# Retention followed by an MLP, fp32 on one core: two chunks of retention ahead of the first products, stages skewed, rounding later, another order at the tail

## The chip, the cores and the metric

The kernel runs on one core of a Trainium2 chip. The metric is the device time of one execution in microseconds (us); three runs of the kernel before are given. A core has a matmul engine (PE, with its weight loads shown apart as PEld), a vector engine (DVE), a scalar engine (ACT), GpSimd (POOL) and a sync engine (SP), which here only issues DMAs. Each engine works through its own instructions in order; semaphores order the engines among each other.

## What is computed

A causal retention (attention without softmax, with a decay per head) over 8 batches x 8 heads x 576 positions x 64, whose output, heads side by side, is a matrix x of 4608 tokens x 512. It goes through an MLP with 2048 hidden units:

```python
scores = (1/sqrt(64)) * q @ k.T                       # per batch and head
Dmat   = where(rel >= 0, gamma[h] ** rel, 0)          # gamma[h] = 1 - 2**(-5-h), rel = i - j
x      = ((scores * Dmat) @ v).transpose(0, 2, 1, 3).reshape(4608, 512)
h      = x @ w_in                                     # (4608, 2048)
g      = h * erf(softplus(h))
out    = g @ w_out                                    # (4608, 512)
```

All inputs and the output are float32 where the kernel sees them, except that the two weights arrive as 64-bit floats, whose words the kernel rounds to float32 itself.

## The kernel before, in words

**Retention.** Each batch's 576 positions are cut into pieces of 128, 128, 128, 128 and 64 rows: 40 pieces in all, numbered through. `load(i)` (L107) issues three DMAs on SP's queue for q, k and v of a piece (256 KB each, rows of 64 floats), into pools of 4 buffers. A piece goes through three stages, each a function:

- `transposes(i)`: pops the loaded piece, issues `load(i+3)`, has POOL weigh v of the next piece with its decay (`weigh_values(i+1)`, L252), transposes q and k on PE through an identity (four transposes each, L267), and copies each from PSUM to SBUF on ACT (L269): qT, kT.
- `scores(i)`: 8 score products on PE (L278), and on DVE the causal mask, two instructions into sT (L91, `sT<-s`).
- `outputs(i)`: 8 products sT x v (L290); for pieces that aren't the first of their batch 4 products of q with the running state (L300); for pieces that aren't the last of it 8 products k x v (L312), added to the state by DVE (L91, or copied by ACT at L324 for a batch's first piece). DVE then scales the result into x (L338, four instructions).

All PSUM tiles of these stages come from one pool of four buffers, `ps_at`, so a stage also waits until whoever read the buffer's last content is done. The list `stages` is worked off by `attend`. Its order is transposes(0), scores(0), then for each i: transposes(i+1), outputs(i), scores(i+1).

**Chunks and products.** The tokens are worked on in 9 chunks of 512, the hidden units in 4 groups (g); that gives 36 (g, c) blocks. A block has a `First` (x times w_in) and a `Second` (times w_out). Both use a Strassen-like scheme with 7 half-size products instead of 8, each of four 128x128 by 128x256 float32 matmuls (8 records in the trace). Their operands are sums: `operands_x` makes four sums of x on DVE for a chunk and stores them to DRAM for the later groups (L382); `First.sums` makes the sums of the activations; `sums_in` and `sums_out` make the sums of the weights. `First` runs in the steps first (products A11, A12), middle (S2, S3, S1), last (S4, A22, then Softplus on ACT), `erf` (ACT) and `multiply` (DVE). `Second` runs first (B11, B21), middle (T2, T3, T1) and last (B22, T4), adds its products into the output tile o on DVE, and stores the two halves of the chunk (`store`, L532 for the last group, L529 for the others).

**Weights.** A part is a DMA of 512 KB (L179, 4 buffers). Group 0 has four parts of w_in and four of w_out. Rounding a part is a generator of steps: two ACT instructions (L196, L197); DVE L201; DVE L205; DVE L209; and DVE L214 with two POOL instructions (L215 multiplies, L216 adds), after which the next part's DMA is issued. After the last part of four come four sums of the group on DVE, which need POOL's addition. `round_weights(n)` runs n steps at the place where it is called, so the calls in the main program set where these instructions stand in each engine's order.

**Order.** The order of all instructions is that in which the program issues them (a manual schedule). Before the first product the program runs the stages until chunk 0 is complete (pieces 0 to 3), with two rounding steps after each stage from the second on. Then the seven products of block 0 run with two stages each, then blocks with one stage per product, up to a limit `most` on how far the stages may be ahead. At the end, when no `First` is left, `erf`, middle, last, `multiply`, `sums` and the last `Second` follow.

Of the kernel before, what the change touches and what calls it, by code (L numbers as in the profile page):

```python
# [46 lines left out]
def kernel(  # L47
# [52 lines left out]
    def load(i):  # L100
        if i >= len(pieces):
            return
        b, s0, n = pieces[i]
        t = {}
        for name, src in (("q", q), ("k", k), ("v", v)):
            t[name] = raw.tile([P, H, D], FP32, tag=name, name=f"raw_{name}")
            nc.sync.dma_start(out=t[name][:n], in_=src[b, :, s0 : s0 + n, :].rearrange("h p d -> p h d"))  # L107
        loaded[i] = t

# [6 lines left out]
    gk, gq, gs, tri = (cst[:, a:b] for a, b in zip(ends, ends[1:]))  # L116
    gk = gk.rearrange("p (s h) -> p s h", s=NS)
    gq = gq.rearrange("p (a i) -> p a i", a=NP)
    load(1)
    load(2)  # L120

# [14 lines left out]
    def parts():  # L136


        w2 = w_in.rearrange("(c p) (h f) -> p c h f", p=P, h=2)
        for g in range(n_g):  # L140
            for dc in range(n_dc):
                a = A11 if dc < 2 else A12
                src = w2[:, dc, :, 2 * g * GW : 2 * (g + 1) * GW]
                yield src, "wa", g, a, dc % 2, sums_in if dc == n_dc - 1 else None
            for f in range(2):
                for j in range(GP):
                    ft = f * FH // P + g * GP + j
                    src = w_out[ft * P : (ft + 1) * P, :].rearrange("p (h o) -> p h o", h=2)
                    yield src, "wb", g, B21 if f else B11, j, sums_out if (f, j) == (1, GP - 1) else None

    def sums_in(a11, s3, a12, a22, s1, s2, s4):
        tt(s1, s3, a22, ALU.add)
        yield
        tt(s2, s1, a11, ALU.subtract)
        yield
        tt(s3, a11, s3, ALU.subtract)
        yield
        tt(s4, a12, s2, ALU.subtract)
        yield

    def sums_out(b11, t3, b21, b22, t1, t2, t4):
        tt(t1, t3, b11, ALU.subtract)
        yield
        tt(t2, b22, t1, ALU.subtract)
        yield
        tt(t3, b22, t3, ALU.subtract)
        yield
        tt(t4, b21, t2, ALU.subtract)
        yield

# [11 lines left out]
    def rounding():  # L182


        while words:
            while words[0][2] > most_g[0]:
                yield
            t, name, g, slot, j, sums = words.pop(0)
            w = operands(name, g)
            dst = w[:, slot : slot + 2, j, :]  # L190
            pairs = t[:, :].rearrange("p (h f two) -> p h f two", h=2, two=2)
            pairs_f = t[:, :].bitcast(FP32).rearrange("p (h f two) -> p h f two", h=2, two=2)
            low, high = pairs[:, :, :, 0], pairs[:, :, :, 1]
            r_f, high_f = pairs_f[:, :, :, 0], pairs_f[:, :, :, 1]
            a_f, a = dst, dst.bitcast(UINT32)
            nc.scalar.activation(a_f, high_f, AF.Abs)  # L196
# [19 lines left out]
            nc.gpsimd.tensor_tensor(out=a_f, in0=a_f, in1=r_f, op=ALU.add)  # L216
            load_weights()
            yield
            if sums:
                yield from sums(*(w[:, i] for i in range(7)))  # L220

    for _ in range(4):
        load_weights()
    round_step = rounding()

# [1 line left out]
        for _ in range(n):  # L227
            next(round_step, None)

    ident = cpool.tile([P, P], FP32, name="ident")  # L230
    make_identity(nc, ident)

    states = [cpool.tile([P, NP, P], FP32, name=f"state{j}") for j in range(2)]
    for t in states:
# [24 lines left out]
    def transposes(i):  # L259
        n = pieces[i][2]  # L260
        t = live[i] = loaded.pop(i)
        load(i + 3)
        weigh_values(i + 1)
        for name in "qk":
            pt = ps_at.tile([P, NP, P], FP32, tag="at", name=f"pt_{name}")
            for p in range(NP):
                nc.tensor.transpose(pt[:, p, :n], flat(t[name][:n, 2 * p : 2 * p + 2, :]), ident[:n, :n])  # L267
            t[name + "T"] = att.tile([P, NP, P], FP32, tag=name + "T", name=name + "T")
            nc.scalar.copy(out=t[name + "T"][:, :, :n], in_=pt[:, :, :n])  # L269

    def scores(i):
# [85 lines left out]
    def stages_for(tokens):  # L357
# [99 lines left out]
    class Second:  # L457


        def __init__(self, first):  # L460
            self.of = first
            self.g, self.c = first.g, first.c

        def begin(self):
            self.o = opool.tile([P, 2, 2, D_MODEL], FP32, tag="o", name="o")
# [61 lines left out]
        def store(self, half):  # L527
            if self.g < n_g - 1:
                nc.sync.dma_start(out=od[self.c][:, half], in_=self.o[:, half])  # L529
            else:  # L530
                r0 = self.c * TCH + half * TH
                nc.sync.dma_start(  # L532
                    out=out[r0 : r0 + TH, :].rearrange("(tp p) o -> p tp o", p=P), in_=self.o[:, half]
                )

    order = [(g, c) for g in range(n_g) for c in range(n_ch)]
# [17 lines left out]

    def run(steps, rounds=(), stages=1):

# [83 lines left out]
```

## Time and profile before

| | us |
|---|---|
| three runs | 1096.83, 1097.54, 1098.64 |
| median | 1097.54 |
| profiled execution | 1099.01 |
| span of its instructions | 1097.2 |

| engine | busy us | share of the span |
|---|---|---|
| PE | 1067.0 | 97% |
| PEld (weight loads) | 918.6 | 84% |
| DVE | 618.7 | 56% |
| ACT | 413.2 | 38% |
| POOL | 120.3 | 11% |

The chain of waits that ended last is PE for 90% of the span. Rows of the profile name a source line, an engine, an operation and "tile written <- tiles read", then partitions x elements and the count. A row in order of time starts with its start and its length in us and ends with the idle time of its engine just before it and what ended that. A row of stretches gives the stretch, its length, the busy time of PE, PEld, DVE, ACT and POOL with the number of instructions, the granted clock of PE (1.00 is full), the busy share of the 16 DMA engines (transfers overlap, so it can pass 1) and GB/s. A row of waits gives engine, tile and line, what ended the wait, then the total in us, the number of waits and the longest. L91 is a helper for all tensor-tensor operations of DVE, so there the tile's name counts.

### The profile page before, as it was taken

How to read it: one execution, taken by the hardware profiler on the slowest of the kernel's cores; microseconds unless marked ns; L12 is line 12 of the kernel's file. 1: busy time of each engine (PE TensorE's matmuls, PEld its weight loads, DVE VectorE, ACT ScalarE, POOL GpSimd, SP SyncE). 2: the span in 40 equal slices, each digit the busy share in tenths (PEclk: the TensorE clock that was granted, in tenths of full speed). 3: DMA queues.
4: the chain of work that ended last, by engine and by line, in shares of the span. 5: the costliest groups of instructions: out<-in, count | busy, mean ns of one | idle time of the engine just before them, and what ended most of it. 6: DMA issues, size and time to landing. Idle time of an engine off the chain costs nothing.

```text
span 1097.2 us, 15487 instructions
## 1 busy us (share of the span) xinstructions
PE 1067.0 (97%) x6400; PEld 918.6 (84%) x6400; DVE 618.7 (56%) x1060; ACT 413.2 (38%) x539; POOL 120.3 (11%) x110
## 2 busy tenths in 40 slices
PE   6798999999999999999999999999999999999997
PEld 5686888888888888888888888888888888888885
DVE  3748657576566664455656555565565445445444
ACT  3244433414334134543344344433344433333340
POOL 3323221111111000010000100100011000000000
PEclk8899999999999999999999999999999999999999
DMA  9767466572663343354455543445454333455432
GB/s 242 202 126 195 122 165 156 129 206 90 166 183 83 125 157 141 144 182 163 185 202 208 208 157 145 182 165 205 179 204 149 144 144 144 170 184 193 172 116 76
DMA packets 141126, 178.57 MB, mean 163 GB/s; under 512 B 115200, under 2 KB 115200, under 8 KB 132992
## 3 DMA queue, kind: packets, MB, share of 16 engines
q1 hardware_dynamic: 140912, 177.23, 49.8%
q8 instruction: 50, 0.82, 0.3%
q10 hardware_dynamic: 144, 0.36, 0.1%
q14 instruction: 20, 0.16, 0.0%
HBM read 123.30 MB, written 54.26 MB: 162 GB/s over the span
## 4 chain that ended last, share of the span: by engine, by line
PE 90%; DVE 0%; issue 0%
PE a L473 23%; PE a L394 22%; PE g L473 11%; PE g L394 11%; PE e L473 6%; PE e L394 5%; PE s L278 3%; PE o L290 2%; PE o L300 2%; PE kv L312 1%; PE pt_q L267 1%; PE pt_k L267 1%; DVE o L91 0%; DVE t L91 0%
## 5 line engine op out<-in xcount | busy, mean ns | idle before, releaser
L394 PE MATMUL a<-x,wa 128*128 128x256 f32 x1152 | 276.9, 383 | 0.0
L394 PEld LDWEIGHTS a<-x,wa 128*128 128x128 f32 x1152 | 218.0, 191 | 30.9 <-issue 0.4
L473 PE MATMUL a<-wb,s 128*128 128x256 f32 x864 | 205.8, 381 | 1.6 <-DVE o L91 1.6
L473 PEld LDWEIGHTS a<-wb,s 128*128 128x128 f32 x864 | 162.6, 190 | 25.0 <-DVE o L91 2.4
L91 DVE TENSOR_TENSOR t<-g,t 128x512 f32<-128x512 f32 x72 | 49.7, 691 | 164.0 <-ACT t L424 119.0
L394 PE MATMUL g<-x,wa 128*128 128x256 f32 x576 | 137.2, 381 | 0.0
L91 DVE TENSOR_TENSOR o<-a,o 128x512 f32<-128x512 f32 x108 | 74.2, 687 | 107.0 <-PE a L473 105.2
L394 PEld LDWEIGHTS g<-x,wa 128*128 128x128 f32 x576 | 108.2, 190 | 14.8
L419 ACT COPY t<-a 128x512 f32<-128x512 f32 x36 | 21.1, 585 | 195.7 <-PE a L394 195.7
L215 POOL TENSOR_TENSOR wraw<-wraw 128x512 f32<-128x512 f32 x32 | 34.0, 1063 | 547.5 <-PE a L394 202.8
L91 DVE TENSOR_TENSOR t<-t,s 128x1024 f32<-128x1024 f32 x72 | 86.4, 1241 | 0.0
L436 ACT ACTIVATE s<-t 128x1024 f32<-128x1024 f32 x72 | 72.1, 1048 | 27.9 <-DVE t L91 27.9
L430 ACT COPY t<-a 128x512 f32<-128x512 f32 x36 | 21.1, 586 | 151.2 <-PE a L394 151.2
L473 PE MATMUL e<-wb,t 128*128 128x256 f32 x288 | 70.5, 388 | 3.8 <-POOL wb L216 3.8
L441 ACT ACTIVATE s<-s 128x1024 f32<-128x1024 f32 x72 | 72.1, 1049 | 0.4
L473 PE MATMUL a<-wb,t 128*128 128x256 f32 x288 | 69.6, 385 | 1.9 <-DVE t L91 1.9
L394 PE MATMUL e<-x,wa 128*128 128x256 f32 x288 | 68.6, 381 | 0.0
L473 PE MATMUL g<-wb,t 128*128 128x256 f32 x288 | 68.6, 381 | 0.0
L473 PE MATMUL g<-wb,s 128*128 128x256 f32 x288 | 68.5, 380 | 0.0
L473 PEld LDWEIGHTS e<-wb,t 128*128 128x128 f32 x288 | 55.3, 194 | 12.0 <-POOL wb L216 4.2
L252 POOL TENSOR_TENSOR raw_v<-raw_v,cst 128x512 f32<-128x512 f32 (+1 forms) x40 | 44.7, 1123 | 170.1 <-DMA raw_v<-in_v_dram 161.8
L473 PEld LDWEIGHTS a<-wb,t 128*128 128x128 f32 x288 | 54.5, 192 | 9.9 <-DVE t L91 2.3
(58 smaller groups left out, 1244.0 us busy)
## 6 DMA issues: line engine op xcount, KB each, us to landing
x<-xd SPq DMA_DIRECT2D x27, 1792.0 KB, 10.8
od<-o SPq DMA_DIRECT2D x54, 512.0 KB, 3.8
o<-od SPq DMA_DIRECT2D x27, 1024.0 KB, 7.0
xd<-x SPq DMA_DIRECT2D x9, 1792.0 KB, 7.0
out_dram<-o SPq DMA_DIRECT2D x18, 512.0 KB, 2.8
raw_q<-in_q_dram SPq DMA_DIRECT2D x32, 256.0 KB, 5.2
raw_k<-in_k_dram SPq DMA_DIRECT2D x32, 256.0 KB, 5.2
raw_v<-in_v_dram SPq DMA_DIRECT2D x32, 256.0 KB, 4.5
```

The source lines that it names most:

```text
L91: nc.vector.tensor_tensor(out=out, in0=in0, in1=in1, op=op)
L215: nc.gpsimd.tensor_tensor(out=r_f, in0=high_f, in1=r_f, op=ALU.mult)
L252: nc.gpsimd.tensor_tensor(out=t[:n], in0=t[:n], in1=gk[:n, s0 // P, :].unsqueeze(2).to_broadcast([n, H, D]), op=ALU.mult,)
L267: nc.tensor.transpose(pt[:, p, :n], flat(t[name][:n, 2 * p : 2 * p + 2, :]), ident[:n, :n])
L278: nc.tensor.matmul(ps[e][:n, p, :n], lhsT=t["kT"][r, p, :n], rhs=t["qT"][r, p, :n], start=True, stop=True)
L290: nc.tensor.matmul(o[e * D : (e + 1) * D, p, :n], lhsT=t["v"][:n, 2 * p + e, :], rhs=t["sT"][:n, e, p, :n], start=(p == 0), stop=(s0 == 0 ...
L300: nc.tensor.matmul(o[:, p, :n], lhsT=kept["state"][:, p, :], rhs=t["qT"][:, p, :n], start=False, stop=(p == NP - 1), skip_group_check=True,)
L394: nc.tensor.matmul(acc[:, j * TH : (j + 1) * TH], lhsT=weights["wa", self.g][:, a, d, j * P : (j + 1) * P], rhs=x[self.g, self.c][a][:, d, :],
L419: nc.scalar.copy(out=self.t1[:, 1], in_=self.a)
L436: nc.scalar.activation(self.s[:, j], t, AF.Softplus)
L441: nc.scalar.activation(self.s[:, j], self.s[:, j], AF.Erf)
L473: nc.tensor.matmul(acc[:, tp, :], lhsT=left[:, j * TH + tp * P : j * TH + (tp + 1) * P], rhs=weights["wb", self.g][:, b, j, :], start=(sta ...
```

## The change

Five things change; the arithmetic is the same except that the weight sums are made in two halves.

1. Stages: the list becomes, for each i from -2 on, transposes(i+2), scores(i+1), outputs(i). The loads move from `transposes` to the end of `outputs`, five pieces ahead; q has 4 buffers, k and v 5, qT 3. Pieces 0 to 3 are loaded at the start, piece 4 in transposes(0).
2. The main program runs the stages until all but outputs(8) of the first two chunks is issued (29 stages), then block 0 without stages between its products.
3. Rounding: two weights instead of four are loaded ahead, two more after outputs(0) and outputs(1); the steps begin after the eleventh stage. The parts of a group come in another order, the sums are made per half (four instructions of 256 columns after every second part) in two steps instead of four.
4. Twelve transposes of the identity (by itself) into an unused PSUM tile stand ahead of everything on PE.
5. Tail: in the second-last block `multiply` comes ahead of the last two products; the very last block stores the right half of its second half early, the left half at the end.

```diff
@@ load
-            t[name] = raw.tile([P, H, D], FP32, tag=name, name=f"raw_{name}")
+            t[name] = raw.tile([P, H, D], FP32, tag=name, name=f"raw_{name}", bufs=4 if name == "q" else 5)
...
-    load(1)
-    load(2)
+    ident = cpool.tile([P, P], FP32, name="ident")
+    make_identity(nc, ident)
+    for i in range(1, 4):
+        load(i)
@@ parts
-            for dc in range(n_dc):
-                a = A11 if dc < 2 else A12
-                src = w2[:, dc, :, 2 * g * GW : 2 * (g + 1) * GW]
-                yield src, "wa", g, a, dc % 2, sums_in if dc == n_dc - 1 else None
-            for f in range(2):
-                for j in range(GP):
+            for j in range(2):
+                for d in range(2):
+                    src = w2[:, 2 * d + j, :, 2 * g * GW : 2 * (g + 1) * GW]
+                    yield src, "wa", g, A12 if d else A11, j, sums_in if d else None
+            for j in range(GP):
+                for f in range(2):
                     ft = f * FH // P + g * GP + j
                     src = w_out[ft * P : (ft + 1) * P, :].rearrange("p (h o) -> p h o", h=2)
-                    yield src, "wb", g, B21 if f else B11, j, sums_out if (f, j) == (1, GP - 1) else None
+                    yield src, "wb", g, B21 if f else B11, j, sums_out if f else None
@@ sums_in, sums_out: a step after every second instruction instead of after each
@@ rounding
-                yield from sums(*(w[:, i] for i in range(7)))
+                yield from sums(*(w[:, i, j, :] for i in range(7)))
-    for _ in range(4):
+    for _ in range(2):
         load_weights()
@@ transposes
-        load(i + 3)
+        if i == 0:
+            load(4)
...
-            t[name + "T"] = att.tile([P, NP, P], FP32, tag=name + "T", name=name + "T")
+            t[name + "T"] = att.tile([P, NP, P], FP32, tag=name + "T", name=name + "T", bufs=3 if name == "q" else 2)
@@ outputs, at its end
+        load(i + 5)
+        if i < 2:
+            load_weights()
@@ stages
-    stages = [(transposes, 0), (scores, 0)]
-    for i in range(len(pieces)):
-        if i + 1 < len(pieces):
-            stages.append((transposes, i + 1))
-        stages.append((outputs, i))
-        if i + 1 < len(pieces):
-            stages.append((scores, i + 1))
+    stages = []
+    for i in range(-2, len(pieces)):
+        for of, piece in ((transposes, i + 2), (scores, i + 1), (outputs, i)):
+            if 0 <= piece < len(pieces):
+                stages.append((of, piece))
@@ Second.last and Second.store
             self.store(0)
+            if self.end:
+                self.store(1, slice(OH, D_MODEL))
             yield
             self.product(T4, self.e, False)
             self.add(1, 0, self.e)
-            self.store(1)
+            self.store(1, slice(0, OH if self.end else D_MODEL))
@@ main program
+    idle = ps_at.tile([P, NP, P], FP32, tag="at", name="idle")
+    for j in range(12):
+        nc.tensor.transpose(idle[:, j % NP, :], ident, ident)
     weigh_values(0)
-    while done[0] < stages_for(TCH):
+    while done[0] < stages_for(2 * TCH) - 1:
         attend(done[0] + 1)
-        if done[0] >= 2:
+        if done[0] > 10:
             round_weights(2)
     operands_x(0, 0)
-    most = [stages_for(2 * TCH) - 1]
+    most = [done[0]]
...
-    run(firsts[0].first(), (0, 1), 2)
-    run(firsts[0].middle(), (0, 1, 2), 2)
-    run(firsts[0].last(), (0, 1), 2)
+    run(firsts[0].first(), (0, 1))
+    run(firsts[0].middle(), (0, 1, 2))
+    run(firsts[0].last(), (0, 1))
+    attend(stages_for(2 * TCH))
+    most[0] = stages_for(3 * TCH) - 1
     firsts[0].erf()
-    most[0] = stages_for(3 * TCH) - 1
-    attend(stages_for(2 * TCH))
     operands_x(0, 1)
-    round_weights(4)
+    round_weights(2)
     run(firsts[1].first(), (0, 1))
+    round_weights(2)
     firsts[0].multiply()
-    round_weights(4)
...
-                round_weights(9)
+                round_weights(6)
...
             run(b.middle())
+            firsts[n + 1].multiply()
             run(b.last())
-            firsts[n + 1].multiply()
             firsts[n + 1].sums()
             run(nxt.first())
```

More of the change, by code (lines that the diff above doesn't have):

```diff
@@ L140, in parts @@
         for g in range(n_g):
-            for dc in range(n_dc):
-                a = A11 if dc < 2 else A12
-                src = w2[:, dc, :, 2 * g * GW : 2 * (g + 1) * GW]
-                yield src, "wa", g, a, dc % 2, sums_in if dc == n_dc - 1 else None
-            for f in range(2):
-                for j in range(GP):
+            for j in range(2):
[4 more added lines that the diff above has]
+                for f in range(2):
                     ft = f * FH // P + g * GP + j
                     src = w_out[ft * P : (ft + 1) * P, :].rearrange("p (h o) -> p h o", h=2)
-                    yield src, "wb", g, B21 if f else B11, j, sums_out if (f, j) == (1, GP - 1) else None
+                    yield src, "wb", g, B21 if f else B11, j, sums_out if f else None
     def sums_in(a11, s3, a12, a22, s1, s2, s4):
         tt(s1, s3, a22, ALU.add)
-        yield
         tt(s2, s1, a11, ALU.subtract)
@@ L156, in sums_in @@
         tt(s3, a11, s3, ALU.subtract)
-        yield
         tt(s4, a12, s2, ALU.subtract)
@@ L162, in sums_out @@
         tt(t1, t3, b11, ALU.subtract)
-        yield
         tt(t2, b22, t1, ALU.subtract)
@@ L166, in sums_out @@
         tt(t3, b22, t3, ALU.subtract)
-        yield
         tt(t4, b21, t2, ALU.subtract)
@@ L228, in round_weights @@
             next(round_step, None)
-    ident = cpool.tile([P, P], FP32, name="ident")
-    make_identity(nc, ident)
     states = [cpool.tile([P, NP, P], FP32, name=f"state{j}") for j in range(2)]
@@ L462, in __init__ @@
             self.g, self.c = first.g, first.c
+            self.end = (self.g, self.c) == (n_g - 1, n_ch - 1)
         def begin(self):
@@ L523, in last, with store @@
             self.add(1, 0, self.e)
-            self.store(1)
+            self.store(1, slice(0, OH if self.end else D_MODEL))
             yield
-        def store(self, half):
+        def store(self, half, os=slice(0, D_MODEL)):
             if self.g < n_g - 1:
-                nc.sync.dma_start(out=od[self.c][:, half], in_=self.o[:, half])
+                nc.sync.dma_start(out=od[self.c][:, half, :, os], in_=self.o[:, half, :, os])
             else:
@@ L532, in store @@
                 nc.sync.dma_start(
-                    out=out[r0 : r0 + TH, :].rearrange("(tp p) o -> p tp o", p=P), in_=self.o[:, half]
+                    out=out[r0 : r0 + TH, os].rearrange("(tp p) o -> p tp o", p=P), in_=self.o[:, half, :, os]
                 )
```

## The prediction

> **What bounds the kernel now.** I read the stretches of the span first (busy time of each engine, granted clock, DMA share, GB/s), since an average over the span hides where PE stands still.
>
> ```profile
> 0.00:5.50 5.50, 0.00 (x0) 0.03 (x1) 0.97 (x2) 1.28 (x1) 0.70 (x6) 1.00 0.71 166
> 5.50:24.00 18.50, 13.34 (x104) 11.27 (x104) 7.21 (x15) 6.90 (x14) 5.46 (x5) 0.82 1.23 265
> 24.00:37.00 13.00, 10.28 (x130) 8.21 (x126) 10.19 (x25) 3.70 (x8) 6.79 (x6) 1.00 1.05 230
> 37.00:50.00 13.00, 9.35 (x74) 7.32 (x69) 10.27 (x18) 2.90 (x5) 5.83 (x5) 0.87 0.55 129
> 50.00:60.00 10.00, 9.99 (x76) 8.70 (x78) 3.27 (x9) 1.56 (x3) 0.00 (x0) 0.66 1.04 275
> 60.00:97.00 37.00, 36.48 (x350) 30.40 (x346) 25.64 (x56) 16.82 (x27) 9.46 (x9) 1.00 0.62 158
> 97.00:114.00 17.00, 12.49 (x85) 9.85 (x84) 13.73 (x29) 5.60 (x12) 8.85 (x8) 0.80 0.49 116
> 114.00:1070.00 956.00, 956.00 (x5528) 827.66 (x5526) 535.10 (x893) 372.51 (x473) 83.21 (x73) 1.00 0.48 163
> 1070.00:1097.20 27.20, 19.05 (x77) 15.18 (x75) 12.37 (x17) 1.93 (x2) 0.00 (x0) 0.90 0.20 77
> ```
>
> From 114 to 1070 us PE is busy 956.0 of 956.0 us at full clock: nothing but less PE work could shorten that. Only the ends can give. Up to 114 us PE idles 22.1 us (length less PE busy, summed) and loses 11.8 us to the clock (length times what the clock lacks of 1.00); in the last 27.2 us it idles 8.2 and loses 2.7. The waits of PE say on what:
>
> ```profile
> PE pt_q L267 <- DMA raw_q<-in_q_dram: 5.5, 1, 5.5
> PE s L278 <- ACT kT L269: 5.1, 2, 4.5
> PE o L290 <- DVE sT L91: 4.4, 4, 2.6
> PE e L473 <- POOL wb L216: 3.8, 1, 3.8
> PE a L473 <- DVE t L91: 1.9, 1, 1.9
> ```
>
> The rows in order of time (start, length, idle before) tell the rest:
>
> ```profile
> 16.60 0.66 ACT L196 ACTIVATE wa<-wraw 128x512 f32<-128x512 f32 x1 [8.25 <-DMA wraw<-in_moe_w_in_dram]
> 18.82 2.08 PE L278 MATMUL s<-qT,kT 64*128 64x128 f32 x16 [4.46 <-ACT kT L269]
> 24.15 1.16 PE L300 MATMUL o<-qT,state 128*128 128x128 f32 x8
> 37.67 2.08 PE L300 MATMUL o<-qT,state 128*128 128x128 f32 x8
> 40.05 2.96 DVE L91 TENSOR_TENSOR wa<-wa 128x512 f32<-128x512 f32 x2 [2.56 <-POOL wa L216]
> 1077.45 2.97 PE L473 MATMUL a<-wb,t 128*128 128x256 f32 x8 [1.92 <-DVE t L91]
> ```
>
> ACT sits in front of a weight that has not landed, and the copies of q and k queue behind it. The same eight L300 matmuls take 1.16 us at full clock, 2.08 at half. And a sum of weights holds DVE until POOL has finished the rounding.
>
> **The change, part by part.** I measure the start by one mark: when PE has done the work that the changed kernel has behind it at the third product (S2) of chunk 0. That is transposes of pieces 0 to 10, scores 0 to 9, outputs 0 to 7, two products. Full-clock prices, start to start, from the rows between 62 and 72 us: transposes 0.95 (half piece 0.55), scores 1.09 (0.62), outputs 2.72 (1.7 without state, 1.75 for a half piece), a product 1.73. Sum: 9x0.95+2x0.55 + 8x1.09+2x0.62 + 5x2.72+2x1.7+1.75 + 2x1.73 = 9.6+10.0+18.8+3.5 = 41.8 us. Before has done 30.9 us of this at 60.49 (6 1/2 transposes, 5 1/2 scores, outputs 0 to 5, three products, same prices) and then runs dense, so it reaches 41.8 at about 71.8.
>
> *Loads.* In the first 33 us raw pieces move at about 218 GB/s: 786 KB in 3.6 us; weights at 390: 524 KB in 1.35 us. The loads go from the transposes to the end of the outputs, two weights instead of four go ahead, and piece 3 moves ahead of them. A new load waits on SP for kv of its piece (its k buffer), and a weight load, once its slot is reused, for POOL's addition of two parts earlier, with the next three raw loads behind it. By my table k of piece 8 lands at 40.5 and is wanted at 44: hidden. Without that cover it costs its lateness one for one. The 4.46 us of ACT's wait go: rounding starts at the eleventh stage, when its weight has been there for 3 us.
>
> *Skew.* The tile order puts outputs(i), transposes(i+3), scores(i+2) between scores(i+1) and outputs(i+1). So sT (1.29) has 4.8 us of cover instead of 0.95, and the waits on sT and x inside a slot go. PE alone would need 4.75 us a slot, DMA 3.6 and a weight's 1.35.
>
> *DVE.* It becomes the next thing late. A slot costs it 1.29 (sT) + 0.87 (state) + 1.13 (x) = 3.3 us, and six rounding steps: 0.42+0.42+0.69+0.43 = 1.96 for a part, and now four half-width sums of 0.37 = 1.5 after each second part. Two slots, twelve steps: 6.6+3.9+1.5 = 12.0, against 9.5 of PE. Each sum also waits for POOL, 1.04+1.30 = 2.4 us (the 2.56 above): 14.4. The sum comes right behind the last rounding step, in a transposes stage, so nothing covers it; behind it on DVE stands sT, and behind that the next transposes, which need that PSUM buffer. Walking the order with these lengths: scores(3) end at 24.1; the three sums end at 39.3, 51.7 and 66.1 (PE stalls of 2.6, 3.5 and 3 us); sT(9) and a step 67.3; two of the four operand sums of x 1.4: S2 starts at 68.7.
>
> *Clock.* That walk has PE at full clock. Before, 5.5 to 24 us are mostly at half. Starting cold would move scores(3), and all DVE work after it, by up to 4 us; POOL running beside DVE stretches some 0.42 us steps to 0.9. The bounds are 0 and +4; I take +2, in the middle, since the row nearest to a pre-phase in full swing (24 to 37 us) is at 1.00 and the nearest to its beginning is not. The twelve dummy transpositions (about 1.1 us for four at half clock, so 3.3 us, between 1.4 and 5.5, when PE idles) cost nothing; they are worth something in these bounds. No row of transposes alone shows the clock. The Trainium skill, "TensorE: Matmul & The Clock Gate", Part 4, says that transposes don't count as busy for the clock: by it the dummies warm nothing and the sum would be 2 us worse, 1089; if they warm, 1085. The same page's list "Why this matters for your kernels" fears only idle gaps over some 3 us; the 2.08 us row at 37.67 follows gaps of 1.02 at most, so the row speaks against relying on it, and my slots of 7 us with 4.75 us of work resemble that row. By the page the walk stays warm (1085).
>
> First term: 68.7+2-71.8 = -1.1 us.
>
> *Behind the mark.* Before loses 0.5+4.5 of idle and 3.4 of clock until 114: 8.4. The 3.8 us wait for wb goes: its last part is rounded at about 91 and wanted at 98 (cover 7 us). The changed kernel pays for S2's idle time with a cold product (3.45 instead of 1.99 at 54.75, about 1.7 with the next) and for DVE's queue of operand sums, the last weight sum, sT(10) and multiply (88 to 98 us) some 1.5 us. Term: 3.2-8.4 = -5.2.
>
> *Undisturbed products.* Five products of block 0 have no attention between them: 1.99 after a stage, 1.73 among products; about 0.2 each: -1.0. From there to 1070 the same work remains; any skew there hides behind 100% PE.
>
> *Tail.* Multiply moves ahead of the last two products: the wait (1.92) and the half clock after it (2.97-1.89 and 2.64-1.89 = 1.8) go, 3.7. The DVE order then puts four sums (2.6) ahead of the take of the first product: that take ends at 1079.6, PE is free at 1079.0, so 0.6 comes back, and the third product starts 2.9 us earlier than its 1082.5. The last store is halved; between nothing and the 0.68 us that 256 KB take at 386 GB/s, 0.5. Term: -3.4.
>
> Sum: -1.1-5.2-1.0-3.4 = -10.7. The span is 1097.2, the profiled execution 1099.0, the median of the runs 1097.54; what lies around the span is untouched, so from the median: 1086.8, say 1087.
>
> **The rivals.** *DVE keeps up (22%).* If sums find POOL done, three times 2.4 us go: S2 at 61.5+2, the sum 1079.6; with DMA and PE alone as bounds (first product 51.6, S2 at 55.1) 1071. For it: DVE idles in every stretch before. Against: the 2.56 us wait is there once in before, for the very same step. Between these two I price it at 1077.
>
> *The clock stays at half through the pre-phase (11%, slower).* PE at 66% load between DVE's waits is cold as at 37.67; half-clock rows are 1.85 times as long (2.0 to 1.09 for scores): 38.4x1.85 = 71 us from about 7.5, two products at 3.2: S2 at 85, 13.2 late. Less 9.6 of the other terms: +3.6, 1101. It decides if S2 starts after 81.4. Against: 24 to 37 us ran at 1.00 with PE 79% busy.
>
> *The wait only moves (16%).* The change doesn't give what it is said to: S2 comes no earlier than 71.8, and the seconds' first product waits for multiply or wb as before. Then the tail alone counts, and a little: 1093. For it: DVE's queue at 88 to 98 us is as full as before's at 98 to 108. Against: wb is 7 us ahead.
>
> **How the numbers follow.** Forecast 51%, rivals as above. The first holds 1081 to 1092 by its unknown costs (cold start 0 to 4, POOL's waits, tail store). The range 1073 to 1097 leaves out the slow clock (about 10%) and the full floor (about 7%). About 0.2% (2.2 us) is what a measurement of this kernel can tell from no change; faster by more: 0.51+0.22+0.11 = 0.84; within it 0.05, from the moved wait; slower 0.11, from the clock.
>
> **What would show it.** Right: PE's waits lose ACT kT and POOL wb; DVE has waits of about 2.4 us on POOL at some 37, 50 and 64 us, each followed by PE waiting for sT; S2 starts at 67 to 73 us after a gap of about 4 us; the last block's first product follows the one before it without a gap; between 114 and 1070 PE is as full as before. Wrong: PE gaps on raw loads in the pre-phase, PEclk at half beyond 25 us, or S2 before 62.

## The result, and the profile after

The changed kernel takes 1099.30 us (median of 6 runs, 1097.58 to 1101.12), the kernel before 1098.57 us (median of 6, the three runs above among them, 1096.83 to 1099.65). The ratio is 1.0009, 95% interval 0.9995 to 1.0024: no change that can be measured. The profiled execution took 1101.12 us, its span 1099.3 us, 2.1 us more than the span before (1097.2).

The stretches of the changed kernel (columns as before: stretch, length, PE, PEld, DVE, ACT, POOL busy, granted clock, DMA share, GB/s):

```profile
24.00:37.00 13.00, 12.23 (x129) 10.57 (x130) 7.13 (x16) 4.09 (x8) 3.64 (x4) 0.74 1.03 232
37.00:50.00 13.00, 8.84 (x70) 7.46 (x71) 10.26 (x23) 4.51 (x8) 6.46 (x6) 0.69 0.87 192
50.00:60.00 10.00, 7.96 (x102) 6.71 (x100) 7.29 (x14) 3.08 (x6) 5.79 (x5) 0.90 0.60 128
60.00:70.00 10.00, 7.95 (x64) 6.82 (x64) 9.01 (x20) 1.88 (x4) 3.50 (x3) 0.66 0.63 137
70.00:80.00 10.00, 5.46 (x44) 4.36 (x40) 7.44 (x17) 2.83 (x5) 3.38 (x3) 0.97 0.80 184
80.00:97.00 17.00, 16.09 (x86) 13.07 (x87) 7.17 (x16) 7.40 (x9) 2.33 (x2) 0.82 0.52 172
97.00:114.00 17.00, 16.31 (x131) 13.43 (x132) 14.60 (x31) 8.75 (x15) 5.17 (x5) 1.00 0.58 178
114.00:1070.00 956.00, 954.74 (x5538) 826.64 (x5534) 542.02 (x926) 368.65 (x469) 84.16 (x74) 1.00 0.49 163
1070.00:1099.30 29.30, 22.55 (x101) 18.57 (x100) 13.57 (x19) 6.55 (x6) 0.00 (x0) 1.00 0.20 72
```

From 24 to 80 us PE is idle for 13.6 of 56 us (length less busy, summed), and its clock is at 0.66 to 0.74 in three of the five stretches. What was dense before (60 to 97 us: 36.48 of 37 us at 1.00) is no longer so. The largest waits of PE in the first 100 us say on what (total, number, longest):

```profile
PE pt_q L264 <- DMA raw_q<-in_q_dram: 4.7, 3, 2.1
PE a L393 <- DVE x L91: 4.5, 1, 4.5
PE pt_q L264 <- DVE sT L91: 3.7, 1, 3.7
PE s L275 <- DVE state L91: 2.4, 1, 2.4
```

Over the whole span, the waits on ACT's kT (5.1) and on POOL's wb (3.8) are gone, and the tail's wait on t with them. DVE now holds PE three times for 2.4 to 4.5 us; before, four waits on its sT made 4.4 us together. DVE's own waits for POOL, in the same stretch:

```profile
DVE wa L91 <- POOL wa L214: 5.2, 2, 2.6
DVE wb L91 <- POOL wb L214: 2.3, 1, 2.3
```

In order of time (start, length, idle before and what ended it):

```profile
24.32 0.43 PE L264 MATMUL pt_q<-ident,raw_q 64*128 64x64 f32 x4 [2.06 <-DMA raw_q<-in_q_dram]
...
29.41 2.08 PE L297 MATMUL o<-qT,state 128*128 128x128 f32 x8
...
37.81 1.35 POOL L214 TENSOR_TENSOR wa<-wa,wraw 128x512 f32<-128x512 f32 x1
...
38.05 1.40 DVE L203 TENSOR_SCALAR wa<-wa 128x512 uint32<-128x512 uint32 x1
...
41.31 0.68 DVE L207 SCALAR_TENSOR_TENSOR wa<-wraw,wa 128x512 uint32<-128x512 uint32 x1
42.02 0.43 DVE L212 TENSOR_SCALAR wraw<-wa 128x512 uint32<-128x512 uint32 x1
45.02 2.38 DVE L91 TENSOR_TENSOR wa<-wa 128x256 f32<-128x256 f32 x4 [2.58 <-POOL wa L214]
47.32 1.28 DVE L91 TENSOR_TENSOR sT<-s,cst 128x512 f32<-128x512 f32 x2
...
58.88 2.37 DVE L91 TENSOR_TENSOR wa<-wa 128x256 f32<-128x256 f32 x4 [2.58 <-POOL wa L214]
...
61.91 0.46 PE L264 MATMUL pt_q<-ident,raw_q 64*128 64x64 f32 x4 [3.68 <-DVE sT L91]
...
80.24 3.75 PE L393 MATMUL a<-x,wa 128*128 128x256 f32 x8 [4.54 <-DVE x L91]
83.78 3.08 PE L393 MATMUL g<-x,wa 128*128 128x256 f32 x8
...
1077.03 1.99 PE L473 MATMUL a<-wb,s 128*128 128x256 f32 x8 [0.78 <-DVE o L91]
...
1080.58 1.89 PE L473 MATMUL a<-wb,t 128*128 128x256 f32 x8
```

Read 41.31 to 47.32: DVE does its last rounding step (L212), then stands for 2.58 us until POOL has multiplied and added, then makes the sum, and only then the mask (sT) that PE needs. It is so three times, and the third time S2 comes behind it, at 80.24, with a cold clock (granted 0.50 there; 3.75 us). In the tail the product of 1080.58 follows without a gap at 1.89 us, where before there were 1.92 us of idle and 2.97.

The chain that ended last confirms it. Before, 90% of it was PE; now it leaves PE at each of the three waits, here at the first (start, length, engine, tile, line):

```profile
42.58 1.04 POOL wraw L213
43.70 1.30 POOL wa L214
45.02 1.26 DVE wa L91
46.30 1.10 DVE wa L91 x3
47.40 0.61 DVE sT L91
48.06 2.67 PE s L275 x16
```

Three marks account for the 2.1 us between the two profiled executions. S2 is at the same amount of PE work at which the kernel before was at about 71.8: +8.4. From there to the first product of the last `Second.last` of the block before the last (B22, at 1077.03 and before at 1071.81): 996.8 instead of 1000.0, -3.2. From there to the end: 22.3 (1077.03 to 1099.3) instead of 25.4, -3.1. The first mark is high: the profiled execution of the changed kernel took 1.8 us more than its median, that of the kernel before 0.4 more. The run without the twelve dummies below, equal to the changed kernel in time, has S2 at 77.65 in an execution of 1098.66 us, and from S2 to the end the two take 1019.1 and 1019.2 us. So such differences lie ahead of S2, and at the medians the first mark is about +7 instead of +8.4 (an estimate from these times).

### The profile page after: what moved, and what is told of

Same layout as the page of the kernel before. It is cut to its first block, busy times and chain, and to the rows that moved or that the text cites. A ratio compares the mean times of both kernels' runs of the same rounds, so it can differ in the third digit from the quotient of the medians.

```text
span 1099.3 us, 15554 instructions
## 1 busy us (share of the span) xinstructions
PE 1069.7 (97%) x6412; PEld 922.3 (84%) x6412; DVE 625.9 (57%) x1092; ACT 414.3 (38%) x539; POOL 119.3 (11%) x110
## 4 chain that ended last, share of the span: by engine, by line
PE 92%; DVE 2%; ACT 2%; SPq 1%; POOL 1%; issue 1%; DMA 1%; POOLq 0%; DVEq 0%; ACTq 0%
PE a L473 23%; PE a L393 22%; PE g L473 12%; PE g L393 11%; PE e L473 6%; PE e L393 5%; PE s L275 3%; PE o L287 3%; PE o L297 3%; PE kv L309 1%; SPq L107 1%; PE pt_q L264 1%; PE pt_k L264 1%; DMA raw_k<-in_k_dram 1%; DVE wa L91 1%
## 5 line engine op out<-in xcount | busy, mean ns | idle before, releaser
L473 PE MATMUL g<-wb,s 128*128 128x256 f32 x288 | 68.7, 381 | 0.0
L91 DVE TENSOR_TENSOR sT<-s,cst 128x512 f32<-128x512 f32 (+1 forms) x80 | 47.0, 628 | 32.6 <-PE s L275 32.4
L473 PEld LDWEIGHTS g<-wb,s 128*128 128x128 f32 x288 | 54.2, 190 | 7.6
## 6 DMA issues: line engine op xcount, KB each, us to landing
x<-xd SPq DMA_DIRECT2D x27, 1792.0 KB, 10.9
```

The costliest lines, as they stand in the source:

```text
L91: nc.vector.tensor_tensor(out=out, in0=in0, in1=in1, op=op)
L473: nc.tensor.matmul(acc[:, tp, :], lhsT=left[:, j * TH + tp * P : j * TH + (tp + 1) * P], rhs=weights["wb", self.g][:, b, j, :], start=(sta ...
```

## The experiments

Ratios are to the kernel before, run on the same chip; edits are to the changed kernel unless said otherwise. Differences between two edited kernels are differences of ratios times 1098.6 us, and are good to some 2 to 3 us. Places in time are those of one profiled execution each, and can be off by as much. The changed kernel stands at 1.0009.

**The tail alone**, in the kernel before.

```diff
@@ before: main program, Second.last, Second.store
+            firsts[n + 1].multiply()   # ahead of b.last(), which followed b.middle()
+            if self.end:
+                self.store(1, slice(OH, D_MODEL))
...
+            self.store(1, slice(0, OH if self.end else D_MODEL))   # at the end, was self.store(1)
```

> The kernel before with the tail part of the change alone. In the changed kernel's trace the last stretch, from the start of product B22 of the second-last block to the end, is 22.3 us against 25.4 before (1077.03 to 1099.3, 1071.81 to 1097.2). If the tail part is worth what it seems there, this kernel is 3.1 us faster than the one before and nothing ahead of 1070 us moves. If the tail gain only came from a different clock phase in that one profile, it is 0 to 1.5 us.

Measured: 1096.54 us, 0.9973 (0.9964 to 0.9982), by the ratio 3.0 us faster than the kernel before. The tail's gain is real, and the rest of the change takes it back.

**Sums one part later**: a sum is made behind the third step of the next part, when POOL is long done.

```diff
-                yield from sums(*(w[:, i, j, :] for i in range(7)))
+                late = sums(*(w[:, i, j, :] for i in range(7)))
@@ behind the third step (L203) of the next part
+            if late is not None:
+                yield from late
+                late = None
...   # only the last sum of a group stays where it was
```

> The changed kernel with the weight sums of the second, fourth and sixth part moved behind the third rounding step of the next part, so that POOL's addition has time to finish. Theory A (the pre-phase is paced by DVE waiting for POOL): the three waits of 2.6, 2.6 and 2.3 us go, product S2 of chunk 0 starts 6 to 8 us earlier than its 80.2, the time falls by 5 to 8 us. Theory B (the half clock of PE paces it): the waits go, but PE's cold stages take their place, S2 moves by under 3 us, the time by under 2. Theory C (late loads): S2 moves by 3 to 5 us at most, since the first 3.4 us were lost before the first rounding step.

Measured: 1091.42 us, 0.9933 (0.9912 to 0.9955), 8.3 us less than the changed kernel (its four runs spread from 1089.4 to 1093.8 us). The edit also moves the last two instructions of the third sum (0.75 us) behind the operands of S2. All waits of DVE for POOL up to S2 are gone, and S2 starts 5.1 us earlier, still behind a wait and cold:

```profile
75.11 3.59 PE L400 MATMUL a<-x,wa 128*128 128x256 f32 x8 [3.33 <-DVE x L91]
```

**Weights later**: the first two weights are loaded behind piece 4 instead of ahead of it.

```diff
-    for _ in range(2):
-        load_weights()
@@ transposes
             load(4)
+            load_weights()
+            load_weights()
```

> The changed kernel with the first two weights loaded behind piece 4 instead of ahead of it. Theory C (the loads of piece 4 come late because of the weights, and shift all that follows): the wait of 2.1 us for q of piece 4 goes, scores of piece 3 end at about 25 instead of 27.6, S2 starts 2 to 4 us earlier, the time falls by 2 to 4 us. Theories A and B: scores of piece 3 move as well, but the chain behind it absorbs it, S2 moves by under 1 us.

Measured: 1096.72 us, 0.9982 (0.9972 to 0.9992), 3.0 us less than the changed kernel. PE no longer waits for piece 4. scores(3) start at 23.25 instead of 25.35, S2 at 76.27 behind the same 4.54 us; DVE's waits for POOL stay (5.1 and 2.3). So the load order is a cost of its own. In the eight traces with two chunks ahead and the first two weights ahead of piece 4, PE waits 1.65 to 4.06 us for q of piece 4 in seven; in the four with the weights behind it, never.

**Dummy transpositions ahead of S2**: 24, at the place where PE waits for x.

```diff
+            if (self.g, self.c) == (0, 0):
+                for n in (8, 8, 4, 4):
+                    fill = ps_at.tile([P, NP, P], FP32, tag="at", name="fill")
+                    for j in range(n):
+                        nc.tensor.transpose(fill[:, j % NP, :], ident, ident)
```

> The changed kernel with 24 dummy transposes ahead of product S2 of chunk 0, where PE waits 4.5 us for the operand sums. Theory B, in its part behind the wait: products S2 and S3 run at full clock (1.9 us each instead of 3.75 and 3.08), the time falls by about 3 us. If transposes don't hold the clock up, S2 and S3 stay at 3 to 3.8 us and the time stays within 0.5 us.

Measured: 1096.38 us, 0.9981 (0.9970 to 0.9992), 3.1 us less than the changed kernel. In order of time:

```profile
74.27 1.91 PE L421 MATMUL fill<-ident 128*128 128x128 f32 x16
76.89 1.09 PE L421 MATMUL fill<-ident 128*128 128x128 f32 x8 [0.72 <-DVE sT L91]
78.98 1.97 PE L393 MATMUL a<-x,wa 128*128 128x256 f32 x8 [0.99 <-DVE x L91]
80.78 1.89 PE L393 MATMUL g<-x,wa 128*128 128x256 f32 x8
```

S2 starts 8.27 us after the first product in both kernels (70.71 here, 71.97 there), and S2 and S3 take 3.86 us where they took 6.83 (3.75 and 3.08): 3.0 us, the whole gain. The cold clock behind the wait is a third cost, apart from the wait itself.

**One chunk ahead**, as before, with rounding from the fourth stage and two stages per product in block 0.

```diff
-    while done[0] < stages_for(2 * TCH) - 1:
+    while done[0] < stages_for(TCH):
         attend(done[0] + 1)
-        if done[0] > 10:
+        if done[0] > 3:
@@ and run(..., 2) in block 0, round_weights(4) twice behind it
```

> The changed kernel with one chunk of retention ahead of the first products instead of two (two stages for each product of block 0 as before; rounding from the fourth stage on); skew, loads, halved sums, dummies and tail as in the change. If running two chunks ahead is itself what costs (all rounding packed into a stretch in which PE has nothing else to do), the products of block 0 cover the waits for POOL and this kernel is 3 to 8 us faster than the changed one. If two chunks ahead is neutral or a gain that the POOL waits only hide, it is within 2 us of it or slower.

Measured: 1095.55 us, 0.9971 (0.9960 to 0.9982), 4.2 us less than the changed kernel. The waits that the second chunk had removed come back behind the first products:

```profile
PE pt_q L264 <- ACT state L321: 5.9, 1, 5.9
PE e L473 <- POOL wb L214: 3.4, 1, 3.4
PE a L473 <- POOL wb L214: 1.9, 1, 1.9
```

So the second chunk does spare these waits, but as it was built it costs more than they do. The run doesn't show that two chunks cost anything by themselves: its first two sums also wait 0 and 0.64 us for POOL instead of 2.58 each, and a run below with two chunks and other places for the sums is 6.7 us faster than this one. And 0.9971 is what the tail alone gives (0.9973): with one chunk, the rest of the change adds nothing that can be measured.

**POOL's rounding done by DVE**, in group 0.

```diff
-            nc.gpsimd.tensor_tensor(out=r_f, in0=high_f, in1=r_f, op=ALU.mult)
-            nc.gpsimd.tensor_tensor(out=a_f, in0=a_f, in1=r_f, op=ALU.add)
+            eng = nc.vector if g == 0 else nc.gpsimd
+            eng.tensor_tensor(out=r_f, in0=high_f, in1=r_f, op=ALU.mult)
+            eng.tensor_tensor(out=a_f, in0=a_f, in1=r_f, op=ALU.add)
```

> The changed kernel with POOL's multiplication and addition of the rounding done by DVE for the first group's eight parts (0.65 us each, 1.3 a part). This takes away both DVE's waits for POOL (7.5 us up to S2) and the stretching of DVE's short rounding steps beside POOL (0.42 to 1.4 us, about 1 us a part, 6 us), and adds 7 x 1.3 = 9 us of DVE work. Theory A in the wide form (waits and stretching): S2 starts 3 to 5 us earlier than its 80.2, the time falls by 2 to 5. If stretching does not count and only the waits do, S2 comes 0 to 2 us later and the time rises by 0 to 2.

Measured: 1094.59 us, 0.9959 (0.9946 to 0.9973), 5.5 us less than the changed kernel, though DVE does more. Up to 100 us no wait of DVE on POOL is left, and L203, seen by its line from 20 to 84 us (shortest, median, longest in ns), no longer stretches; first this run, then the changed kernel:

```profile
L203 DVE TENSOR_SCALAR wa<-wa x4: 416/423/428, 33.6 to 53.4; 128x512 uint32<-128x512 uint32 x4
```

```profile
L203 DVE TENSOR_SCALAR wa<-wa x4: 410/905/1395, 34.2 to 52.8; 128x512 uint32<-128x512 uint32 x4
```

S2 starts at 76.73. This fits the wide form of the theory, waits and stretching; by the expectation, with the waits alone the time would not have fallen. Some other steps of DVE are still stretched here beside POOL's weighing of v (L207 takes 1.48 us at 40.73 instead of 0.69).

**Without the twelve dummies** at the start.

```diff
-    idle = ps_at.tile([P, NP, P], FP32, tag="at", name="idle")
-    for j in range(12):
-        nc.tensor.transpose(idle[:, j % NP, :], ident, ident)
```

> The changed kernel without the twelve dummy transposes at the start. With them the first transposes of q and k ran at full clock (0.66 us for four), without them in the kernel before at half (1.09). Everything behind waits for the load of piece 1 until 8.7 us, so whatever the dummies do to the clock, it is used up there: the time stays within 0.5 us. If the clock they win lasts, this kernel is 1 to 3 us slower than the changed one.

Measured: 1099.14 us, 1.0008 (0.9997 to 1.0019): they are worth nothing in time. On the clock they act in some executions. The first rows of this run, then of the changed kernel, then of the run with dummies ahead of S2, which has the same twelve at the start:

```profile
5.41 1.09 PE L264 MATMUL pt_q<-ident,raw_q 128*128 128x128 f32 x4 [5.41 <-DMA raw_q<-in_q_dram]
...
8.92 1.11 PE L264 MATMUL pt_q<-ident,raw_q 128*128 128x128 f32 x4 [1.29 <-DMA raw_q<-in_q_dram]
```

```profile
5.05 0.66 PE L264 MATMUL pt_q<-ident,raw_q 128*128 128x128 f32 x4 [0.87 <-DMA raw_q<-in_q_dram]
...
8.66 1.12 PE L264 MATMUL pt_q<-ident,raw_q 128*128 128x128 f32 x4 [1.76 <-DMA raw_q<-in_q_dram]
```

```profile
5.23 1.11 PE L264 MATMUL pt_q<-ident,raw_q 128*128 128x128 f32 x4 [1.05 <-DMA raw_q<-in_q_dram]
```

Of the twelve traces with the dummies, the first transposes of q take 0.66 us in three (the changed kernel's among them) and 1.11 to 1.12 in nine; in the three without them 1.08 to 1.09. The transposes of the next piece wait for their data anyway and are cold either way.

**The three remedies together**: sums later, weights later, 24 transpositions ahead of S2 (the diffs above).

> The changed kernel with the three edits together: later sums, first two weights behind piece 4, 24 dummy transposes ahead of S2. Alone they took off 8.3, 2.9 and 3.0 us (by their ratios). If they remove different losses, the sum is about 13 us against the changed kernel (1085 to 1088); if weights and clock only share the same wait with the sums, it is 8 to 10 (1089 to 1092).

Measured: 1087.57 us, 0.9899 (0.9884 to 0.9914), 12.1 us less than the changed kernel where the single gains add up to 14.4, and faster than both kernels. S2 starts at 71.32 after 0.72 us of waiting.

**Rounding from the seventh stage on**, the same 38 steps ahead of S2.

```diff
-        if done[0] > 10:
-            round_weights(2)
+        if done[0] > 6:
+            round_weights(2 if done[0] <= 21 else 1)
```

> The changed kernel, with the rounding steps beginning after the seventh stage instead of the eleventh (two after each stage up to the 21st, one after each of the rest). Theory (a sum that waits for POOL right behind the last rounding step stops DVE, wherever the steps stand): the steps are spread over 23 stages instead of 19, the three waits of DVE for POOL stay at 2.3 to 2.6 us each, the third product of chunk 0 starts 1 to 4 us earlier than in the changed kernel (at 76 to 79 us), the ratio to the kernel before is 0.996 to 1.000. Rival (the packing into the last stages is the trouble, not the waits): less work of DVE per stage lets the sums catch up, the third product starts before 74 us, ratio below 0.995. Second rival (rounding later was needed, since the weights land late): ACT waits for a weight again and the copies of q and k behind it, PE has waits on ACT kT or ACT qT of over 2 us, ratio 1.001 or more.

Measured: 1087.83 us, 0.9910 (0.9888 to 0.9933). This one edit does as much as the three remedies. S2 starts at 69.75 at full clock after 0.42 us. My theory (S2 1 to 4 us earlier, at 76 to 79) is refuted, and its "wherever the steps stand" with it; what came is what the first rival forecast for less DVE work per stage (before 74 us, below 0.995). The rows of DVE show that a step's place changed as well:

```profile
43.90 0.68 DVE L207 SCALAR_TENSOR_TENSOR wa<-wraw,wa 128x512 uint32<-128x512 uint32 x1
44.61 1.15 DVE L212 TENSOR_SCALAR wraw<-wa 128x512 uint32<-128x512 uint32 x1
46.04 0.86 DVE L335 SCALAR_TENSOR_TENSOR x<-o,cst 128x64 f32<-128x64 f32 x4 [0.28 <-PE o L297]
48.32 2.38 DVE L91 TENSOR_TENSOR wa<-wa 128x256 f32<-128x256 f32 x4 [1.43 <-POOL wa L214]
```

Between the last rounding step and the sum DVE now scales x: the waits of the first two sums are 0.35 and 1.43 us instead of 2.58 each, that of the third 1.19 instead of 2.29. Two steps a stage and twelve steps for two parts make six stages, so the sums meet the same kind of stage each time: transposes in the changed kernel, where DVE has nothing to do, outputs for the first two here. But the steps also begin earlier and end at a slower pace; two runs take the earlier start and the place apart.

**Later still, sums behind outputs**: the same 38 steps from the 13th stage on, so that the first two sums stand behind outputs(4) and (6), the third behind transposes(10) as in the change.

```diff
-        if done[0] > 10:
-            round_weights(2)
+        if done[0] > 12:
+            round_weights(2 if done[0] in range(13, 25) or done[0] == 29 else 3)
```

> The changed kernel with the rounding begun later still, after the thirteenth stage, two steps after each stage up to the 24th, three after each of the 25th to 28th, two after the 29th: the same 38 steps before the third product. The first two weight sums now stand behind an outputs stage (of pieces 4 and 6), where DVE first adds the state and scales x, some 2 us, instead of behind a transposes stage, where DVE has nothing to do; the third stays behind transposes(10). If the place of the sums in the slot is what counts: the first two waits of DVE for POOL (2.58 each) fall below 1.5 us, two of PE's three waits on sT and state go, the third product starts at 73 to 79 us instead of 80.2, ratio to the kernel before 0.993 to 0.999. If the early start is what counts: the third product starts at 80 us or later, ratio 1.000 to 1.006.

Measured: 1097.48 us, 0.9984 (0.9975 to 0.9994). Rows of DVE and PE:

```profile
59.73 2.38 DVE L91 TENSOR_TENSOR wa<-wa 128x256 f32<-128x256 f32 x4 [0.68 <-POOL wa L214]
...
72.98 1.09 DVE L91 TENSOR_TENSOR wb<-wb 128x256 f32<-128x256 f32 x3 [2.29 <-POOL wb L214]
...
76.54 3.75 PE L393 MATMUL a<-x,wa 128*128 128x256 f32 x8 [6.66 <-DVE x L91]
```

The first two waits fall to 1.80 (not below the 1.5 expected) and 0.68, and A11, the first product, starts at 66.15 instead of 71.97 although rounding began two stages later. But the third sum still waits 2.29 right ahead of the operands of S2, with more steps packed before it, and S2 stands 6.66 us for it: of the 5.8 us at A11, 3.7 remain at S2 (76.54), and 2.7 us in the time.

**Early, sums where the change has them**: from the seventh stage on, one step a stage up to the 14th, then two.

```diff
-        if done[0] > 10:
-            round_weights(2)
+        if done[0] > 6:
+            round_weights(1 if done[0] < 15 else 2)
```

> The changed kernel with the rounding begun after the seventh stage, one step after each stage up to the 14th, then two: from the 16th stage on every step and sum stands where the changed kernel has it, with the three sums behind transposes(6), (8) and (10). If the place of the sums counts: the waits of DVE for POOL stay at 2.3 to 2.6 us, the third product starts at 77 to 81 us, ratio to the kernel before 0.998 to 1.002. If the early start counts: the first sum finds POOL done, the third product starts before 75 us, ratio below 0.995.

Measured: 1097.29 us, 0.9987 (0.9978 to 0.9997).

```profile
41.12 1.55 DVE L91 TENSOR_TENSOR wa<-wa 128x256 f32<-128x256 f32 x4 [2.57 <-POOL wa L214]
...
54.84 2.37 DVE L91 TENSOR_TENSOR wa<-wa 128x256 f32<-128x256 f32 x4 [2.58 <-POOL wa L214]
...
76.46 3.54 PE L393 MATMUL a<-x,wa 128*128 128x256 f32 x8 [4.54 <-DVE x L91]
```

The same start as with the rounding from the seventh stage on, and the waits are back at 2.57, 2.58 and, for the third, 2.30. The early start is worth 2.4 us of that run's 10.9; the other 8.5 come with the place of the three sums, and with the steps' pace, which differs between the two as well (two a stage first and one later, or one first and two later).

**The remedies once more, with another on top.** In group 0 DVE in POOL's place: 

> The run with all three remedies (sums moved behind the next part's third step, weights later, 24 transpositions ahead of the third product), and in group 0 the two rounding instructions of POOL done by DVE. Theory (the waits of DVE for POOL were the main cost, the stretching of DVE's short steps beside POOL a smaller one): with the sums already moved there is no wait left to save; DVE takes on eight times some 1.0 to 1.4 us and saves what the stretching cost, so the ratio to the kernel before is 0.988 to 0.993, the same as without this edit or up to 3 us worse. Rival (the stretching of DVE's steps beside POOL is a main cost of its own): ratio below 0.987, the third product of chunk 0 before 70 us.

Measured: 1088.43 us, 0.9912 (0.9883 to 0.9940). And with rounding from the seventh stage: 

> The run with all three remedies, and the rounding from the seventh stage on (two steps after each stage up to the 21st, one after each of the rest). Theory (with the waits gone the pre-phase is bound by PE at a clock that falls in its gaps and by the loads): moving the steps gains 0 to 2 us more, ratio 0.987 to 0.990, third product of chunk 0 at 69 to 72 us. Rival (DVE's queue is still the bound): the steps' spreading shows in full, ratio below 0.986, third product before 68 us. Second rival (the weights, now loaded later still, are not there): ACT waits for a weight, ratio above 0.992.

Measured: 1087.84 us, 0.9914 (0.9889 to 0.9938). Neither adds anything (in the second, ACT waits 11.0 us for weights, which may have taken back what the spreading gave): four different ways end between 0.9899 and 0.9914, with intervals that overlap. So nothing that was tried beyond that helped. DVE isn't thereby cleared: in the run with DVE in POOL's place, PE's longest waits up to 75 us are still on DVE (4.9 us for sT, 4.1 for the state). What bounds these four at their start stays open.

## Why the prediction was wrong

*The first term* failed: -1.1 was forecast, +8.4 came in the profiled execution (about +7 at the medians), and these 9.5 us are most of the error. Its working named the mechanism (a sum right behind the last rounding step waits 2.4 us for POOL, nothing covers it, sT and the next transposes stand behind it), and the waits came at that size (2.58, 2.58, 2.29). What it mis-sized was the walk around them, which priced PE at full clock, DVE's steps unstretched and the early loads as hidden. In the profiled execution S2 came at 80.24 (some 1.8 us earlier at the median, by the estimate above); the walk had 68.7 before its allowance of 2, so 11.5 us were missing there:

- *Loads and the start*, 3.5: scores(3) ended at 27.6, not 24.1. The prediction had checked the load of piece 8 and not that of piece 4, which came 2.06 late for PE (24.32) because two weights went ahead of it; scores(3) then ran cold. The run with weights later gives 3.0 us back.
- *From there to the end of the first sum*, 4.6 (19.8 instead of 15.2). PE ran cold from 25.5 to 31.4, at a granted clock of 0.50 (2.08 for the eight L297 that take 1.16; with the outputs before them 1.8 us). DVE's steps stretched beside POOL: L203 took 1.40 instead of 0.42 at 38.05, while POOL's L214 ran from 37.81 to 39.16. And the sum took 2.38 instead of 4x0.37: its first instruction 1.26, beside POOL's weighing of the next v, which stands right behind its addition (44.95 to 45.99). In the run with the early start and the sums where the change has them, with POOL idle for most of it, the first sum took 1.55.
- *The second and third sums*, 1.4 and 2.1: the same stretching (L203 1.39 at 52.81 and at 67.80), and PE cold from 62 to 69.5. How the two divide these times was not measured.

*Clock.* "+2, in the middle" was too little: I used 24 to 37 us of the kernel before (1.00) for a pre-phase whose PE idles 13.6 of 56 us; half clock followed a gap of only 2.06 us (24.32) too. The twelve dummies, said to be worth something in these bounds, were worth nothing. The rival that put the clock at half throughout has the nearest time (1101), but in part by luck: S2 was 8.4 late and not 13.2, and the other terms brought less than it took off. By its own sign, S2 after 81.4, it did not decide, and its mechanism holds only in parts: the clock was 0.66 to 0.74 in three stretches, 0.90 and 0.97 in two. "The wait only moves" names what was seen, S2 no earlier than 71.8; its price was wrong, as it let S2 come exactly where it stood before, and its other half, the wait for wb as before, did not come. Of the signs named for being wrong, two came: PE's gaps on raw loads (4.7 us) and half clock beyond 25 us.

*Behind the mark and the undisturbed products*: -6.2 forecast, -3.2 measured. The waits on wb went as forecast. The cold products behind S2's wait cost 3.0 instead of 1.7 (S3 was cold too, 3.08), and PE idled 0.68, 0.69 and 1.26 us (at 89.27, 107.82 and 125.63), 2.6 where 1.5 had been counted. Some 0.6 us stay unexplained.

*Tail*: -3.4 forecast, -3.1 in the trace, -3.0 by the run of it alone. The halved last store, priced at 0.5, shows no gain: from the end of the last product to the end of the span it is 4.6 us (1094.68 to 1099.3), before 4.7.

*"DVE keeps up"* (1077) did not happen. What the change is worth with the sums' places mended and the other remedies added is 1087.6 to 1088.4. That this is near the forecast of 1087 is luck, since the forecast had the waits in it.

So the gain of the tail (3.0 us) and of the vanished waits was given back by a pre-phase in which PE waits for DVE and DVE for POOL. The runs show the place of the sums as the greater part (8.3 us by moving them behind the next part; 8.5 between two runs that differ in the sums' place and in the steps' pace), load order (3.0) and the cold products behind the last wait (3.1) as the rest. These prices do not simply add: the run with rounding from the seventh stage still waits 3.36 us for piece 4 and is as fast as the three remedies together.

## What to carry to other kernels

An instruction that waits for a slower engine belongs behind other work of its own queue, and with a fixed number of steps per stage the remainder decides which work that is: count it out for each phase before moving a start. When a critical resource is asked to wait repeatedly, price the wait with what it brings along (cold clock, stretched neighbours): here moving three waits of some 2.5 us was worth 8.3 us, give or take 3. Moving work into a stretch where PE has nothing else to do may take away the cover that made it free; no run here shows that by itself.

## What the hardware showed

Transpositions alone can hold PE's clock: over a stall, 24 of them kept two products at 1.97 and 1.89 us that take 3.75 and 3.08 without, and the granted clock at 1.00 instead of 0.50 for the first; in the three other runs with the 24, S2 took 1.89 to 1.96. As a warm-up from a standing start twelve of them (2.82 us) were not reliable: the next ones took 0.66 us in three traces, 1.11 to 1.12 in nine. The Trainium skill, "TensorE: Matmul & The Clock Gate", Part 4, says that transposes don't count as busy for the clock in the same way; the rows of the 24 contradict it for fp32 transposes through an identity.

DVE's single-source step on 128x512 words (L203) took 0.42 us alone and up to 1.40 beside POOL's tensor-tensor operations, ending only when POOL's had ended (38.05 + 1.40 against 37.81 + 1.35, 0.29 us behind; at 52.81 and 67.80 0.28 us behind), and 0.43 at most in the run that took the rounding off POOL. The Trainium skill, "SBUF — State Buffer", section "SBUF: two separate sides", tells of an exclusive lock on a port pair that the two engines share, which a DVE instruction takes in a two-port mode or with two inputs in SBUF; the rows agree with it, though no run here shows the mode, and I had not used it.
